# First chunk of direct attention units in full-height matmuls, 18 direct units for 20, and a new price for zeros in the planner

## Chip, cores and metric

The kernel runs on one core of a Trainium2 chip. The metric is the device time of one execution, in microseconds (us). The engines are PE (TensorE: matmuls; PEld is its weight loads), DVE (VectorE), ACT (ScalarE), POOL (GpSimd) and SP (SyncE, which issues the DMAs).

## The reference

Three layers follow one another: causal attention in blocks of 64, a mixing layer with squared ReLU, and a gated layer with a product over time. All data is float32. Cut to what matters:

```python
def _attn_ref(q, k, v):                       # q, k, v: (4, 8, 576, 64)
    scores = (1.0 / np.sqrt(D)) * np.matmul(q, k.transpose(0, 1, 3, 2))
    mask = (pos[:, None] // 64) >= (pos[None, :] // 64)
    scores = np.where(mask, scores, -1000000000.0)
    attn = softmax(scores)
    return np.matmul(attn, v)

def _moe_ref(x, mu_k, mu_r, w_k, w_v, w_r):   # x: (4, 576, 512), d_ff 1024
    xk = mu_k * x + (1.0 - mu_k) * x_prev
    xr = mu_r * x + (1.0 - mu_r) * x_prev
    k = np.maximum(xk @ w_k, 0.0)
    return sigmoid(xr @ w_r) * (k * k @ w_v)

def _moe2_ref(x, w_in, g_ln, w_sg, b_sg, w_out):
    u, v = split(gelu(x @ w_in))
    v_s = np.einsum('ts,bsd->btd', w_sg, layernorm(v) * g_ln) + b_sg[None, :, None]
    return x + (u * v_s) @ w_out
```

## The kernel before

**Units.** Attention is cut into 64 units: one batch and head, and either its first 320 queries (kind LO, chunks of 64, 128 and 128 queries) or its last 256 (kind HI, two chunks of 128). `CH0`, `CHN` and `CHE` give each chunk's first query, its number of queries, and the keys it can see. Units 0 to 15 are LO of batches 0 and 1, units 16 to 31 HI of the same; then the same for batches 2 and 3. A unit goes through three steps on PE: `emit_S` (scores, into the banks SA, SB or M), `emit_T` (128 by 128 transposes of the softmaxed scores P, into T) and `emit_PV` (product with V, into O). Between them DVE takes maxima (`stats`) and sums (`rr`), ACT scales (`nb`), takes exponentials (P) and copies T out (PH, PL).

**Direct and split units.** A unit n below `DIRECT` is direct: its scores and its value product are float32 matmuls, each of which the chip runs as two passes on PE, so that a float32 matmul stands twice in the trace. The mask is in two extra rows of q and k (66 rows; 128 in the first four units). Its output comes with queries as rows, is scaled by DVE into `otmp`, and for each pair of heads is transposed back by PE (`T<-ident,otmp`). All other units are split: q, k, v and P are cut into two float32r parts (ACT copies the high part, POOL or DVE subtracts), a score takes two one-pass matmuls, the value product ten for HI, and its output needs no transpose back. The first chunk of a LO unit has 64 queries. Rows 64 to 127 of its P are zeroed once at the start.

**The rest.** A moe1 matmul (`M<-xh,w`, `xl`, `kh`, `kl`, 288 columns, two passes of every three by the high part) needs weights that were loaded and converted on ACT, DVE and POOL (`w_split`; tiles u, th, w). In the opening moe1 can only take the channels of batch 0 whose heads are done.

**Order.** The program first lists all operations, then `Plan.schedule` plays them through a model with a duration per operation (`takes`, `preload`) and always takes for an engine the ready operation of lowest rank. Rank is the place in the list plus a bias: `MB` for mixing, `CB` for weight conversion, `SB` for softmax steps, `EV` for copies out of T, `XV` for attention outputs; lower goes earlier. A load of weights on SP waits while the model's DMA backlog is above `BACKLOG` ns. `LEFT` conversions are left for the moe1 loop. The order that comes out is fixed: on the chip each engine runs its list in that order and waits where it must. All engine instructions stand in the profile under line 596, so they are told apart by tiles.

**Fillers.** Where the model sees PE idle for over 300 ns in the first two layers, it puts matmuls of zeros into the list: a plain filler (`O<-calm 64x128`, one pass) when no group of matmuls is open in O, otherwise zeros that are added to the open group (`O<-calm 128x64`, float32, two passes). How many fit is gap over price; the price of one was

```python
f = (n / 2.4 + 6) * x          # n = 128 for a filler, 4 * 64 for zeros; x is 1 or 2
```

They do no work for the result, and once in the list PE runs all of them, needed or not.

Of the kernel before, what the change touches and what calls it, by code (L numbers as in the profile page):

```python
# [9 lines left out]
F32 = mybir.dt.float32  # L10
# [10 lines left out]
CH0 = [0, 64, 192, 320, 448]  # L21
CHN = [64, 128, 128, 128, 128]
# [54 lines left out]


FILL = 128
BACKLOG = 6000  # L80
MORE = 20.0
FILL_DUTY = 1.0
COLD_DUTY = 1.0
# [253 lines left out]
class Plan:  # L337
# [77 lines left out]
    def play(self, rings):  # L415
# [8 lines left out]
        order, opened, began = [], 0, 0.0  # L424
# [42 lines left out]
        while True:  # L467
            best = None
            for e in soon:
# [3 lines left out]
                if ripe[e]:  # L473
                    t = free[e]
# [8 lines left out]
            t, e = best  # L483
# [25 lines left out]
            if e == "NONE":  # L509
                op.run, op.end = (t, t), t  # L510
                if filler and filler.alts[0][2]["out"].tile.pool in op.alts[0][1]:
                    filler = None
            elif op.alts[i][1] == "dma_start":
                a = op.alts[i][2]
                v = next(x for x in a.values() if isinstance(x, View))
                rows = v.shape[0]
                size = v.cols * rows * 4 if not v.tile.dram else v.cols * 4
                t = max(t, lanes.pop(0) + 40)
                if e == "SP":
                    free[e] = t + 375  # L520
                dma = max(t + 1400, dma) + size / (250.0 if rows != 66 else 172.0)
                op.run, op.end = (t, t + 375), dma + 150
                lanes.append(op.end)
            else:
                busy, d, port = takes(e, *op.alts[i][1:])
                if e != "PE":
                    busy, d = busy + MORE, d + MORE
                s = t
                if e == "PE":
                    gap = t - free[e]  # L530
                    s = t = max(t, began + preload(op.alts[i][1], op.alts[i][2]) * (2.0 if gate.slow else 1.0))
                    a = op.alts[i][2]
                    if filler and self.filler_from <= t and gap > (100 if gate.slow else 300):
                        x = gate.step(free[e])
                        more, n = filler, FILL
                        if opened:
                            more, n = zeros(group) if group["out"].cols <= FILL else None, 4 * group["out"].cols
                        f = (n / 2.4 + 6) * x
                        room = gap - max(0, self.filler_from - free[e])
                        k = int(room * COLD_DUTY / f if x > 1 else (room - 100) * (FILL_DUTY if gate.share(t) > AMPLE else 1.0) / f) if more else 0  # L540
                        at = max(free[e], self.filler_from)
                        for _ in range(k):
                            order.insert(len(order) - 1, (more, 0))
                            gate.add(at, min(t, at + n / 2.4 * x))
                            at += f
                    if filler and "out" in a and a["out"].tile is filler.alts[0][2]["out"].tile:
                        opened += bool(a.get("start")) - bool(a.get("stop"))
                        group = a
                    x = gate.step(t)
                    fn, v, ins = op.alts[i][1], a.get("out", a.get("_0")), a.get("lhsT", a.get("_1"))  # L550
                    cols = (v.cols if fn == "matmul" else 60) * (4 if ins.tile.dt == F32 else 1) * ins.shape[0] / 128 / 2.4
                    gate.add(t, t + min(busy, cols) * x)
                    d += busy * (x - 1)
                    busy *= x
                if port:
                    o = "POOL" if e == "DVE" else "DVE"
                    s = max(t, lock[o])
                end = max(s + d, t + d)
                free[e] = max(s + busy, end - (d - busy))
                if port:  # L560
                    lock[e] = end - (150 if e == "DVE" else 0)
                op.run, op.end = (s, free[e]), end
                if e == "PE":
                    began = s
# [34 lines left out]
WHO = dict(oN="A", wl="P", wc="V", Q="A", K="A", Ql="P", Kl="P", V="A", Vl="P", PH="A", O="A", xh="A", xl="P", kh="A", kl="P",  # L599
           X="A", Xl="V", vh="V", vl="V", gU="P", gh="A", gl="V", sg="A", sl="V", R2="A", R="A", P="V", PL="V")  # L600
ALT = 200.0
MB = -300
CB = -200
SB = 0
EV = -200
XV = -200
LO, HI = 0, 1
CHUNKS = [[0, 1, 2], [3, 4]]
TOKENS = [(0, 320), (320, 576)]
# [19 lines left out]
]  # L629


DIRECT = 20
PADDED = 4
SEATS = [("SA", "SBa"), ("M", "M"), ("SBb", "SA"), ("M", "M"), ("SBa", "SBb"), ("SA", "SBa"), ("SBb", "SA"), ("SBa", "SBb"),
         ("SA", "SBa"), ("SBb", "SA"), ("SBa", "SBb"), ("SA", "SBa"), ("SBb", "SA"), ("SBa", "SBb"), ("SA", "SBa"), ("SBb", "SA")]
# [5 lines left out]
W1 = 21  # L641
UT = 2
CONV = 4
LEFT = 12
X0_AT = 0.55
CONV2 = 2

# [6 lines left out]
def fused_kernel(ctx: ExitStack, tc: tile.TileContext, first, later, qkv_lo, qkv_hi, mu,  # L654
# [48 lines left out]
    def mm(out, lhsT, rhs, start=False, stop=False):  # L703
        op = nc.tensor.matmul(out=out, lhsT=lhsT, rhs=rhs, start=start, stop=stop)
        t = out.tile
        if start and t in stopped:
            op.preds[stopped[t].n] = stopped[t]
        if stop:
            stopped[t] = op
# [170 lines left out]
    def emit_S(n):  # L880
        b, h, kind = units[n]
        order.need(("sp", n))
        Q, K, KL = splits.pop(n)
        chunks = CHUNKS[kind]
        if n < DIRECT and kind == LO:
            (sa, ka), (sb, kb) = [ptile(t, 512, PS_BUFS.get(t, 1)) for t in SEATS[n]]
            P = spots[n % 3]
        else:
            (sa, ka), (sb, kb) = ptile("SA", 512, 1), ptile("SB", 1024, 1)
            P = [(pbuf[1 - n % 2], o) for o in POFF]  # L890
        stc = {0: sa[:, 0:64], 1: sa[:, 64:256], 2: sb[:, 0:320], 3: sa[:, 0:448]}
        if kind == HI:
            stc[4] = sb[:, 224:800]
        skc = [ka, ka, kb, ka, kb]
        probs[n] = P
        pe(score_ns(n))
        mx, sm = smax[n % 4], ssum[n % 4]
        t0, t1 = TOKENS[kind]
        nb = atile([128, 5], F32, "nb", 4)
        rr = atile([128, 5], F32, "rr", 4)  # L900
        for c in chunks:
            q0, m, e, st = CH0[c] - TOKENS[kind][0], CHN[c], CHE[c], stc[c]
            for k0, k1 in PIECES[c]:
                o = st[0:m, k0:k1]
                if n < DIRECT:
                    mm(o, Q[:, q0:q0 + m], K[:, k0:k1], start=True, stop=True)
                    continue
                mm(o, Q[:, q0:q0 + m], K[:, k0:k1], start=True)
                mm(o, q2[n % 2][:, CH0[c]:CH0[c] + m], KL[:, k0:k1], stop=True)

        def red(cs):
            for c in cs:
                m, e, st = CHN[c], CHE[c], stc[c]
                nc.vector.tensor_reduce(out=mx[0:m, c:c + 1], in_=st[0:m, 0:e], axis=AX.X, op=ALU.max)
            s = slice(cs[0], cs[-1] + 1)
            nc.scalar.activation(out=nb[:, s], in_=mx[:, s], func=AF.Copy, scale=-0.125)

        def exp(cs):
            for c in cs:
                m, e, st, (p, po) = CHN[c], CHE[c], stc[c], P[c]  # L920
                nc.scalar.activation(out=p[0:m, po:po + e], in_=st[0:m, 0:e], func=AF.Exp,
                                     scale=0.125, bias=nb[0:m, c:c + 1], accum_out=sm[0:m, c, 0:1])

        def norm():
            cs = slice(chunks[0], chunks[-1] + 1)
            nc.vector.tensor_reduce(out=rr[:, cs], in_=sm[:, cs], axis=AX.X, op=ALU.add)
            nc.vector.reciprocal(out=rr[:, cs], in_=rr[:, cs])
            if n < DIRECT:
                scales[n] = rr
                return  # L930
            for c in chunks:
                m, e, (p, o) = CHN[c], CHE[c], P[c]

                p, r = p[0:m, o:o + e], rr[0:m, c:c + 1]
                plan.add(*[("scalar", "activation", dict(out=p, in_=p, func=AF.Copy, scale=r)) if w == "A" else
                           ("vector", "tensor_scalar", dict(out=p, in0=p, scalar1=r, scalar2=None, op0=ALU.mult,
                                                            op1=ALU.add, accum_out=junk[0:m, c:c + 1]))
                           for w in WHO["P"]])

        parts = [[0, 1, 2]] if kind == LO else [[3], [4]]  # L940
        t = 0
        for cs in parts:
            w = sum(CHE[c] for c in cs)
            sk = [skc[c] for c in cs]
            at(t, plan.rank(SB, lambda cs=cs: red(cs)), *sk)
            t += 1.1 * w
            at(t + 100, plan.rank(SB, lambda cs=cs: exp(cs)), *sk, ("P", n))
        at(t + 1.2 * w + 500, plan.rank(SB, norm), ("N" if n < DIRECT else "P", n))
# [39 lines left out]
    def direct_PV(n):  # L988
# [29 lines left out]
        t, tk = ptile("T", 512, 2)  # L1018
        t0, t1 = TOKENS[kind]
        for i, c in enumerate(chunks):  # L1020
            m = CHN[c]
            nc.tensor.transpose(t[:, CH0[c] - t0:CH0[c] - t0 + m], o[0:m, i, :], ident[0:m, 0:m])
        x = new_xt(b, h)
        at(0, plan.rank(XV, lambda: copy("O", x[:, 1 + t0:1 + t1], t[:, 0:t1 - t0])), tk, ("x", b, kind))

# [582 lines left out]
```

## Time and profile before

| | |
|---|---|
| median of 3 timed runs | 694.78 us (694.05 to 695.16) |
| the profiled execution | 693.84 us |
| its span, first to last instruction | 691.9 us |
| PE busy | 684.7 us, 99% of the span |
| PEld (weight loads) busy | 658.2 us, 95% |
| DVE, ACT, POOL busy | 450.8, 453.8, 308.6 us |
| matmul instructions on PE | 5074, with 136 fillers and 54 passes of zeros |

PE counts as busy from a matmul's start to its modelled end, so a busy PE can still be standing while its array empties; the starts of the weight loads show that better. The 1.9 us between span and time lie outside the program's instructions.

### The profile page before, as it was taken

How to read it: one execution, taken by the hardware profiler on the slowest of the kernel's cores; microseconds unless marked ns; L12 is line 12 of the kernel's file. 1: busy time of each engine (PE TensorE's matmuls, PEld its weight loads, DVE VectorE, ACT ScalarE, POOL GpSimd, SP SyncE). 2: the span in 40 equal slices, each digit the busy share in tenths (PEclk: the TensorE clock that was granted, in tenths of full speed). 3: DMA queues.
4: the chain of work that ended last, by engine and by line, in shares of the span. 5: the costliest groups of instructions: out<-in, count | busy, mean ns of one | idle time of the engine just before them, and what ended most of it. 6: DMA issues, size and time to landing. Idle time of an engine off the chain costs nothing.

```text
span 691.9 us, 14054 instructions
## 1 busy us (share of the span) xinstructions
PE 684.7 (99%) x5074; PEld 658.2 (95%) x5074; DVE 450.8 (65%) x1141; ACT 453.8 (66%) x1287; POOL 308.6 (45%) x374
## 2 busy tenths in 40 slices
PE   8999999999999999999999999999999999999998
PEld 6989989999999999999999999999999998998998
DVE  4767787257877766766776877686988257256233
ACT  5779877797998898998898898583452131132120
POOL 4345544665575566667677564240234032032031
PEclk9999999999999999999999999999999999999999
DMA  8564122234322323334332410633900300300102
GB/s 269 203 219 159 35 77 78 86 124 133 110 75 75 115 85 102 89 103 135 96 103 98 137 47 1 240 107 105 323 1 17 121 1 9 129 1 10 61 1 69
DMA packets 34821, 68.24 MB, mean 99 GB/s; under 512 B 6048, under 2 KB 20640, under 8 KB 34752
## 3 DMA queue, kind: packets, MB, share of 16 engines
q1 hardware_dynamic: 34608, 67.34, 30.1%
q8 instruction: 40, 0.66, 0.4%
q14 instruction: 29, 0.24, 0.1%
q10 hardware_dynamic: 144, 0.00, 0.0%
HBM read 54.75 MB, written 9.44 MB: 93 GB/s over the span
## 4 chain that ended last, share of the span: by engine, by line
PE 95%; DVE 2%; ACT 2%; DMA 0%; issue 0%; POOL 0%; POOLq 0%; ACTq 0%
PE M L596 49%; PE O L596 19%; PE T L596 10%; PE V L596 7%; PE SB L596 5%; PE SA L596 5%; ACT P L596 1%; DVE th L596 1%; DMA kh<-first_dram 0%; DVE stats L596 0%; DVE u L596 0%; ACT PH L596 0%; DVE otmp L596 0%; ACT otmp L596 0%; DVE o L596 0%
## 5 line engine op out<-in xcount | busy, mean ns | idle before, releaser
L596 PE MATMUL M<-xh,w 128*128 128x288 f32 x704 | 166.8, 305 | 0.1
L596 PEld LDWEIGHTS M<-xh,w 128*128 128x128 f32 x704 | 119.6, 188 | 1.0 <-ACT R L596 0.3
L596 PE MATMUL M<-xl,w 128*128 128x288 f32 x352 | 104.4, 297 | 0.0
L596 PE MATMUL M<-kh,w 128*128 128x288 f32 x432 | 104.0, 307 | 0.0
L596 POOL TENSOR_TENSOR xl<-t,xh 128x288 fp32r<-128x288 f32 x64 | 53.2, 832 | 58.9 <-ACT xh L596 55.7
L596 POOL TENSOR_TENSOR gt<-gt,U 128x288 f32<-128x288 f32 x32 | 29.5, 925 | 102.1 <-DVE gt L596 52.7
L596 PE MATMUL T<-ident,P 128*128 128x128 f32 x480 | 74.3, 274 | 0.3 <-ACT P L596 0.3
L596 PEld LDWEIGHTS M<-kh,w 128*128 128x128 f32 x432 | 73.6, 188 | 1.0 <-issue 0.6
L596 DVE TENSOR_TENSOR PL<-T,PH 128x320 fp32r<-128x320 f32 (+3 forms) x116 | 61.8, 543 | 17.4 <-ACT PH L596 16.5
L596 ACT ACTIVATE PH<-T 128x384 fp32r<-128x384 f32 (+4 forms) x138 | 63.7, 479 | 12.3 <-PE T L596 11.6
L596 POOL TENSOR_TENSOR kl<-R,kh 128x288 fp32r<-128x288 f32 x64 | 53.6, 840 | 32.4 <-ACT kh L596 31.3
L596 PEld LDWEIGHTS M<-xl,w 128*128 128x128 f32 x352 | 66.3, 188 | 0.3
L596 PE MATMUL M<-kl,w 128*128 128x288 f32 x216 | 63.8, 296 | 0.0
L596 PEld LDWEIGHTS T<-ident,P 128*128 128x128 f32 x480 | 58.0, 141 | 3.1 <-ACT P L596 0.8
L596 ACT ACTIVATE U<-M 128x288 f32<-128x288 f32 x32 | 13.2, 412 | 69.9 <-PE M L596 69.9
L596 DVE TENSOR_SCALAR_CACHE_REDUCE P<-P,rr 128x448 f32<-128x448 f32 (+3 forms) x104 | 58.2, 582 | 0.6
L596 POOL TENSOR_TENSOR k<-qkv,K 64x576 fp32r<-64x576 f32 (+1 forms) x44 | 53.7, 1221 | 4.4 <-ACT K L596 2.3
L596 PE MATMUL O<-gh,w 128*128 128x288 f32 x256 | 51.7, 294 | 0.2 <-DVE o L596 0.2
L596 PE MATMUL M<-XHL,w 128*128 128x288 f32 x384 | 51.7, 294 | 0.0
L596 PEld LDWEIGHTS M<-XHL,w 128*128 128x128 f32 x384 | 51.2, 188 | 0.1
L596 POOL TENSOR_TENSOR Q<-qkv,Q 64x256 fp32r<-64x256 f32 (+1 forms) x44 | 35.0, 794 | 33.2 <-ACT Q L596 20.0
L596 PE MATMUL O<-PH,V 128*128 128x256 f32 (+2 forms) x188 | 47.3, 279 | 0.0
(186 smaller groups left out, 1891.1 us busy)
## 6 DMA issues: line engine op xcount, KB each, us to landing
qkv<-qkv_hi_dram SPq DMA_DIRECT2D x28, 576.0 KB, 3.7
qkv<-qkv_lo_dram SPq DMA_DIRECT2D x16, 416.0 KB, 3.1
x2d<-th SPq DMA_DIRECT2D x32, 144.0 KB, 3.1
X<-x2d SPq DMA_DIRECT2D x4, 1152.0 KB, 5.6
outT_dram<-o SPq DMA_DIRECT2D x32, 144.0 KB, 1.8
w<-w_k_dram SPq DMA_DIRECT2D x8, 512.0 KB, 8.7
w<-w_v_dram SPq DMA_DIRECT2D x8, 512.0 KB, 4.3
w<-w_in_dram SPq DMA_DIRECT2D x8, 512.0 KB, 5.5
```

The costliest lines, as they stand in the source:

```text
L596: getattr(getattr(self.nc, e), fn)(*pos, **{k: real(x) for k, x in a.items() if k[0] != "_"})
```

## The change

The first chunk of a direct LO unit multiplies 128 queries instead of its own 64 (the 64 further rows of scores are not used), and its output is transposed back as 128 by 128 instead of 64 by 64; the extra columns are overwritten by the next chunk's. `DIRECT` falls from 20 to 18, so units 18 and 19 (HI, batch 0, heads 2 and 3) become split. In the planner zeros of this form cost at least 220 ns. Five biases, the DMA backlog and `LEFT` get other values, by which the whole order on all engines comes out anew.

```diff
-BACKLOG = 6000
+BACKLOG = 7500
...
-                        f = (n / 2.4 + 6) * x
+                        f = max(n / 2.4 + 6, 220.0 if opened and group["lhsT"].tile.dt == F32 and group["out"].shape[0] > 64 else 0) * x
...
-MB = -300
-CB = -200
-SB = 0
-EV = -200
-XV = -200
+MB = -200
+CB = -350
+SB = 200
+EV = -50
+XV = -100
...
-DIRECT = 20
+DIRECT = 18
...
-LEFT = 12
+LEFT = 14
...
                 if n < DIRECT:
-                    mm(o, Q[:, q0:q0 + m], K[:, k0:k1], start=True, stop=True)
+                    mm(st[:, k0:k1], Q[:, q0:q0 + 128], K[:, k0:k1], start=True, stop=True)
...
         for i, c in enumerate(chunks):
-            m = CHN[c]
-            nc.tensor.transpose(t[:, CH0[c] - t0:CH0[c] - t0 + m], o[0:m, i, :], ident[0:m, 0:m])
+            nc.tensor.transpose(t[:, CH0[c] - t0:CH0[c] - t0 + 128], o[:, i, :], ident)
```

Three places show how the order moves. The first is PE's list in the opening, around the scores of unit 5 (`SA<-qkv`) and the value product of unit 3 (`O<-kl,PL`); before:

```order
L596 MATMUL SA<-qkv 64x64
L596 MATMUL SA<-qkv 128x192
L596 MATMUL O<-calm 128x64 x8
L596 MATMUL M<-xh,w 128x288 x2
L596 MATMUL O<-kl,PL_315 128x64
L596 MATMUL O<-kl,PL_276 128x64
L596 MATMUL O<-kl,PL_315 128x64 x2
```

and now:

```order
L596 MATMUL SA<-qkv 128x64
L596 MATMUL SA<-qkv 128x192
L596 MATMUL O<-calm 128x64
L596 MATMUL O<-kl,PL_311 128x64
L596 MATMUL O<-kl,PL_278 128x64
L596 MATMUL O<-kl,PL_311 128x64 x2
L596 MATMUL T_167<-ident,P_88 128x128 x3
L596 MATMUL O<-calm 64x128 x18
```

The score has 128 rows, eight zeros have become one, two moe1 matmuls went later, and a run of 18 plain fillers stands after the next transposes. The second place is PE's list ahead of the scores of unit 7 (`SB<-qkv`), whose q, k and v are loaded into a buffer that unit 4's value product frees; before:

```order
L596 MATMUL O<-calm 64x128 x15
L596 MATMUL O<-qkv,PL_541 128x64 x2
L596 MATMUL O<-qkv,PL_543 128x64
L596 MATMUL O<-qkv,PL_541 128x64
L596 MATMUL O<-qkv,PL_543 128x64 x2
L596 MATMUL M<-xh,w 128x288
L596 MATMUL SB<-qkv 64x64
```

and now:

```order
L596 MATMUL O<-calm 64x128 x20
L596 MATMUL T_167<-ident,P_88 128x128 x3
L596 MATMUL O<-qkv,PL_507 128x64 x2
L596 MATMUL O<-calm 128x64
L596 MATMUL O<-qkv,PL_536 128x64
L596 MATMUL O<-qkv,PL_507 128x64
L596 MATMUL O<-qkv,PL_536 128x64 x2
L596 MATMUL O<-calm 64x128 x71
L596 MATMUL SB<-qkv 128x64
```

In place of one moe1 matmul a run of 71 fillers now stands right ahead of unit 7's scores. The third place is DVE's list just before it takes the maxima of the same unit 7 (`stats<-SB`), where `u` and `th` are steps of weight conversion; before:

```order
L596 TENSOR_REDUCE rr<-sums 128x3
L596 RECIPROCAL rr<-rr 128x3
L596 SCALAR_TENSOR_TENSOR u<-w,u 128x512
L596 TENSOR_SCALAR u<-u 128x512
L596 SCALAR_TENSOR_TENSOR u<-w,u 128x512
L596 SCALAR_TENSOR_TENSOR t_538<-xT,mu_t,t_538 128x288
L596 SCALAR_TENSOR_TENSOR u<-w,u 128x512
L596 TENSOR_TENSOR otmp<-O,rr 128x3x64
L596 TENSOR_REDUCE stats<-SB 64x1
```

and now:

```order
L596 TENSOR_TENSOR otmp<-O,rr 128x3x64
L596 TENSOR_SCALAR u<-u 128x512 x2
L596 SCALAR_TENSOR_TENSOR u<-w,u 128x512
L596 TENSOR_SCALAR u<-u 128x512
L596 SCALAR_TENSOR_TENSOR u<-w,u 128x512 x2
L596 TENSOR_SCALAR th<-th 128x512
L596 SCALAR_TENSOR_TENSOR u<-w,u 128x512
L596 TENSOR_REDUCE rr<-sums 128x3
L596 RECIPROCAL rr<-rr 128x3
L596 TENSOR_TENSOR otmp<-O,rr 128x3x64
```

The sums of a unit (`rr<-sums`), which free its output, now stand behind eight conversion steps in a row. Counted over the whole program, PE's list goes from 5074 passes to 5083: 69 more fillers (136 to 205), 42 fewer passes of zeros (54 to 12), 36 fewer passes of direct value products and 12 fewer of direct scores, 12 and 20 more of split scores and value products, and 2 fewer transposes back.

## Rows read from the trace of the kernel before

**Rows 1.** The profile's page: granted clock in 40 slices, 9 is 90% or more
```profile
PEclk9999999999999999999999999999999999999999
```

**Rows 2.** Two stretches: busy us (count) of PE, PEld, DVE, ACT, POOL; clock; DMA
```profile
0.00:62.00 62.00, 59.09 (x466) 51.39 (x466) 39.41 (x110) 44.98 (x141) 25.39 (x46) 1.00 0.70 233
62.00:120.00 58.00, 58.00 (x420) 52.49 (x420) 43.53 (x102) 47.51 (x142) 27.81 (x28) 1.00 0.19 55
```

**Rows 3.** Waits in the first 62 us: us in total, times, longest
```profile
DVE otmp L596 <- PE O L596: 6.1, 7, 2.2
...
DVE stats L596 <- PE SB L596: 4.5, 5, 1.9
...
ACT PH L596 <- PE T L596: 3.4, 4, 1.8
ACT xT L596 <- PE T L596: 3.4, 4, 1.1
```

**Rows 4.** Weight loads around a 64-query score: start us, us, what [idle before]
```profile
18.05 0.14 PEld L596 LDWEIGHTS T<-ident,P 128*128 128x128 f32 x1
...
18.36 0.19 PEld L596 LDWEIGHTS SA<-qkv 66*64 66x64 f32 x2 [0.17 <-issue]
...
18.61 0.19 PEld L596 LDWEIGHTS SA<-qkv 66*128 66x128 f32 x1
```

**Rows 5.** Weight loads: a transpose, then scores of 128 queries on 66 rows
```profile
15.54 0.14 PEld L596 LDWEIGHTS T<-ident,P 128*128 128x128 f32 x1
...
15.64 0.19 PEld L596 LDWEIGHTS SB<-qkv 66*128 66x128 f32 x1
...
15.64 0.30 PEld L596 LDWEIGHTS SB<-qkv 66*128 66x128 f32 x2
```

**Rows 6.** Weight loads around one first-chunk transpose back
```profile
36.09 0.14 PEld L596 LDWEIGHTS T<-ident,P 128*128 128x128 f32 x1
...
36.35 0.14 PEld L596 LDWEIGHTS T<-ident,otmp 64*128 64x128 f32 x1
...
36.72 0.14 PEld L596 LDWEIGHTS T<-ident,P 128*128 128x128 f32 x1
```

**Rows 7.** Timeline of PE: one direct score of 288 keys; direct value products
```profile
96.59 0.65 PE L596 MATMUL SB<-qkv 66*128 66x288 f32 x2
97.08 0.78 PE L596 MATMUL O<-qkv,PL 128*128 128x64 f32 x6
...
134.68 2.12 PE L596 MATMUL O<-qkv,PL 128*128 128x64 f32 x18
```

**Rows 8.** Timeline of PE: scores of a split unit; value product of one
```profile
132.85 0.45 PE L596 MATMUL SA<-K,Q 128*128 128x448 f32 x1
...
133.88 0.30 PE L596 MATMUL M<-xh,w 128*128 128x288 f32 x1
...
150.75 0.28 PE L596 MATMUL O<-PH,V 128*128 128x256 f32 x1
...
151.81 0.28 PE L596 MATMUL O<-PL,V 128*128 128x256 f32 x1
```

**Rows 9.** Zeros on PE: count | busy us, mean ns | idle before
```profile
L596 PE MATMUL O<-calm 128*128 128x64 f32 x54 | 6.8, 272 | 0.0
```

**Rows 10.** Timeline around a run of zeros
```profile
28.60 2.57 PE L596 MATMUL O<-calm 128*128 128x64 f32 x22
...
29.19 0.47 ACT L596 ACTIVATE PL<-T 128x384 f32<-128x384 f32 x1
...
31.00 1.06 PE L596 MATMUL O<-qkv,PL 128*128 128x64 f32 x8
...
32.09 0.36 DVE L596 TENSOR_TENSOR otmp<-O,rr 128x192 f32<-128x192 f32 x1 [2.17 <-PE O L596]
```

**Rows 11.** A run of plain fillers
```profile
25.96 1.05 PE L596 MATMUL O<-calm 128*64 128x128 f32 x14
```

**Rows 12.** VectorE's longest step on weights in the first 62 us
```profile
L596 DVE SCALAR_TENSOR_TENSOR u<-w,u 128x512 int32<-128x512 int32 x12 | 8.9, 748 | 0.0
```

## The prediction

> **What bounds the kernel now.** I read the granted clock first: it is full in all 40 slices [rows 1], so no time hides in a slow TensorE. Then the table by stretches. From 62 to 120 us PE is busy for all 58.00 us, and in the first 62 us for 59.09 [rows 2], while DVE and ACT have 39.41 and 44.98. PE's list is run in order, so the end of the program moves with two things only: how long PE needs for its list at its own pace, and how long it stands for others. In the opening both matter, because fillers make PE look busy where the planner expected it to stand. The waits there show which engine really leads: DVE and ACT stood 6.1, 4.5, 3.4 and 3.4 us for PE (17.4 in these four alone) [rows 3]. From about 62 us on, anything taken out of PE's list is gained at the end unless a new wait takes its place.
>
> A matmul's busy time is of no use for pricing PE, since successive ones overlap. I price by distances between starts.
>
> **The first chunk of scores.** Where a 64-query score follows a transpose, the transpose's weight load starts at 18.05, the score's first at 18.36 after 0.17 us of idle, and the first load of the 192-key score behind it at 18.61 [rows 4]: 0.56 us for three loads (the transpose and two passes). Without a change of shape loads follow each other at 0.10 to 0.11: 15.54, 15.64, and the second of the pair 0.11 later (0.30 less 0.19), and these last are scores of 128 queries on 66 rows straight behind a transpose [rows 5]. With 128 queries the three loads should take 0.33. That is 0.23 us less, 16 times (one per LO unit of batches 0 and 1): 3.7 us. A wider load costs something too: the two narrow ones start some 0.06 us apart (0.19 for both, each 0.13 to 0.14 long), against 0.11; that is already inside the 0.33. Ends of the range: 3.7, and a loss of 1.7 if the idle time stays (32 loads, 0.055 each).
>
> **The transposes back.** From the load of the transpose before (36.09) over the 64-row one (36.35) to the load after the 128-row ones (36.72) is 0.63 us for three loads [rows 6], against 0.33. Here the first load began early, behind a filler, so I take 0.25 and not 0.30. Eight pairs of heads: 2.0 us.
>
> **Two units fewer are direct.** A direct HI unit has a score of 288 keys twice, at 0.49 each (96.59 to 97.08), and one of 448, by columns 0.76; its 18 value passes go at 0.112 each ((2.12 - 0.78)/12) [rows 7], 2.01; and half of a pair's two transposes back, 0.11. Sum 3.86 us. A split unit needs 1.03 for its scores (132.85 to 133.88) and 1.18 for ten value passes (150.75 to 151.81 for nine, and 0.12) [rows 8], 2.21. The difference, 1.65, counts twice: 3.3 us. What the two units add on ACT, DVE, POOL and SP (copies and subtractions of q, k, v, P, and two small DMAs) is what 28 later HI units do already. It lies beside moe1 matmuls that PE can do meanwhile, while DVE is free for 14.5 of 58 us [rows 2]; I cost it at nothing. Without that cover it would be one more step ahead of each unit's scores, some 0.75 us each if it is as long as the step in [rows 12].
>
> **Fillers and zeros.** The trace has 54 passes of zeros [rows 9]; 42 go. In a run of 22 they start 0.11 apart (28.60 to 31.00), and that run shows what they cost when too many: the copy PL that the next product needs was done at 29.66 (29.19 and 0.47), but the product started at 31.00, and DVE stood 2.17 us for it [rows 10]. Plain fillers go at 0.062 ((1.05 - 0.24)/13) [rows 11]; 69 come. So 4.6 us less and 4.3 more: 0.3 us less. The fillers now stand where the planner sees the waits, the largest run, 71 or 4.4 us, ahead of unit 7's scores.
>
> **The sum.** 3.7 + 2.0 + 3.3 + 0.3 = 9.3 us by which PE's list is shorter at its own pace. From the profiled execution, 693.84, that leaves 684.5; its time is 0.94 below the median of 694.78, so 685.5 against the median.
>
> **What is given back.** About 5.5 of these 9.3 us (scores and most transposes back) lie in the opening, where PE then reaches its meeting points earlier than DVE and ACT may be ready. How much comes back as waits no row shows; the bounds are none and all 5.5. I set it by who waited for whom there: PE's share is the time that its list holds for waiting, 136 fillers at 0.062 and 54 zeros at 0.11, 14.3 us, against the 17.4 us that others waited for PE, so 45%, or 2.5 us. This is an estimate. Net gain 6.8 us: 688.0.
>
> **The biases and the backlog** move work between neighbours on every engine but neither add nor remove any. By the order, one more weight load (11 for 10) stands ahead of unit 7's on SP. I cost them at nothing, with the rivals below as their price.
>
> **Rivals.**
> *All of it is gained, and the overrun with it.* For: DVE and ACT were waiting for PE more than the reverse [rows 3], and the run of zeros above wasted 1.3 us on the chain to unit 7's load. Against: the 71 fillers say that the planner expects a wait at the same place. 9.3 to 11 us less: 684 to 685.5, with one more such overrun 683. Chance 0.25.
>
> *The opening is held by others.* If the first units go at the pace of DVE and ACT with their weight conversions, all 5.5 us come back and only 3.8 stay: 691. For: DVE's 39.4 and ACT's 45.0 of 62 us are not far from a dependent chain's limit. Against: the same waits. Chance 0.18.
>
> *The full-height score gains nothing.* If what PE waited for came from the 66 rows and not the 64 columns, the 3.7 go, the wider loads cost 1.7, and 3.9 less about 1 of waits stays: 691.9. Against it stand the 66-row loads without any gap [rows 5]. Chance 0.04. The Trainium skill, "TensorE: Matmul & The Clock Gate", section "LDWEIGHTS (loading the stationary operand)", has a load cost its columns over 1.2 GHz, so 53 ns for 64 and 107 for 128; by that rule alone the change lengthens 32 loads by 1.7 us. The same skill's "TensorEngine Tiling (Array Packing)", section "Key Properties", says that changing the tiling mode drains the array, which speaks for the other reading. The trace agrees with both at once, 0.06 against 0.11 between loads and 0.17 of idle at the change [rows 4, 5]; only for the plain fillers, also 64 columns wide, is no such gap seen: the first load in [rows 6] stands behind one and has no idle time.
>
> *Slower: conversions ahead of the softmax.* DVE now has eight conversion steps in a row ahead of a unit's sums, ACT likewise. One of the long ones takes 0.75 us [rows 12]. PE is in order, so what it stands for at one unit delays everything behind. The gain of 9.3 is used up by 12 such steps that nothing covers, less than one for each of the 16 LO units. One for each is 12 us: 697.5. Against: conversions must be done before moe1 can use PE, so early ones also remove waits; and PE's list holds fillers at these places. Chance 0.08.
>
> *Nothing to be seen,* gains and waits cancelling: 693.4 to 696.2. Chance 0.05.
>
> **How the numbers follow.** The forecast, 685.5 to 690, has 0.40 and is the likeliest; its time is 688.0. A measurement of this kernel tells about 0.2%, 1.4 us, from no change. Faster by more are the forecast and the first three rivals, 0.87, less 0.01 for their upper tails: 0.86; within 0.2% 0.06; slower 0.08. The range reaches down to the full gain with one overrun and up through the opening held by others and the idle score: 682.5 to 692.
>
> **What would show it.** The 66-row scores have one shape, with loads 0.11 apart and no idle time ahead of the first chunk. The transposes back start 0.11 apart. The first split HI scores come two units earlier. By the scores of unit 15, the last LO unit of batch 1, PE is about 3 us ahead; by the end of attention about 3 more. If the waits for PE grow in the first 62 us, the estimate of 2.5 was too large; if PE's own waits for ACT P, DVE otmp or the load of qkv pass 4 us, the opening is held by others. Any slice with a granted clock below 1.00 would make it all wrong.

## The result, and the profile after

The changed kernel takes 687.58 us (median of 4 runs, 686.53 to 687.72) against 694.97 for the kernel before: a ratio of 0.9892, 95% interval 0.9877 to 0.9907, or 7.4 us less. Forecast were 688.0 and 682.5 to 692. The profiled execution took 687.72, its span is 686.0.

The page after, busy shares and granted clock:

```profile
PE 678.2 (99%) x5083; PEld 657.9 (96%) x5083; DVE 459.7 (67%) x1155; ACT 458.5 (67%) x1294; POOL 316.4 (46%) x380
...
PEclk9999999999999999999999999999999999999999
```

Two stretches of it (busy us of PE, PEld, DVE, ACT, POOL; clock; DMA):

```profile
0.00:62.00 62.00, 58.05 (x494) 52.61 (x495) 43.09 (x115) 45.78 (x140) 26.09 (x47) 1.00 0.68 233
62.00:120.00 58.00, 57.47 (x435) 54.65 (x435) 39.15 (x98) 47.27 (x140) 30.91 (x32) 1.00 0.24 72
```

The clock is full throughout, as before [rows 1]. PE is still the bound: 678.2 of 686.0 us. In the first 62 us it is busy less (58.05 for 59.09) and DVE more (43.09 for 39.41) [rows 2].

Weight loads after, around the first chunk of unit 5's scores (start us, us, what):

```profile
18.46 0.14 PEld L596 LDWEIGHTS T<-ident,P 128*128 128x128 f32 x1
...
18.57 0.19 PEld L596 LDWEIGHTS SA<-qkv 66*128 66x128 f32 x1
...
18.68 0.19 PEld L596 LDWEIGHTS SA<-qkv 66*128 66x128 f32 x1
...
18.79 0.19 PEld L596 LDWEIGHTS SA<-qkv 66*128 66x128 f32 x1
```

The transpose's load starts at 18.46, the two of the score at 18.57 and 18.68, the first of the 192-key score at 18.79: 0.33 us for three and no idle time, for 0.56 with 0.17 of idle [rows 4]. A transpose back with what follows it, on PE's timeline after:

```profile
33.29 0.49 PE L596 MATMUL T<-ident,otmp 128*128 128x128 f32 x3
33.62 0.27 PE L596 MATMUL T<-ident,P 128*128 128x128 f32 x1
```

and the same place before:

```profile
36.13 0.29 PE L596 MATMUL T<-ident,P 128*128 128x128 f32 x1
36.35 0.64 PE L596 MATMUL T<-ident,otmp 64*128 64x64 f32 x3
36.83 0.38 PE L596 MATMUL T<-ident,P 128*128 128x128 f32 x2
```

Three matmuls follow each other at 0.11 now (33.29 to 33.62). Before, the four from 36.13 to 36.83 took 0.70, where 0.44 would be the pace: 0.26 less, as priced (0.25), though [rows 6] hold four loads and not three as the prediction counted.

The waits of the opening after:

```profile
ACT nb L596 <- DVE stats L596: 7.4, 4, 4.5
...
DVE otmp L596 <- PE O L596: 3.9, 6, 1.5
DVE stats L596 <- PE SB L596: 3.4, 4, 1.6
...
ACT xT L596 <- PE T L596: 1.1, 2, 0.8
```

DVE and ACT wait less for PE now (3.9, 3.4, 1.1 for 6.1, 4.5, 3.4) [rows 3]; the first line, ACT's wait for DVE's maxima, comes back below. PE's timeline ahead of unit 7's scores:

```profile
37.57 4.48 PE L596 MATMUL O<-calm 128*64 128x128 f32 x71 [0.45 <-DVE otmp L596]
41.89 0.38 PE L596 MATMUL SB<-qkv 66*128 66x64 f32 x2
```

The 71 fillers run from 37.57 for 4.48 us, and the scores start at 41.89. Then comes what the total hides. Where does unit 15, the last LO unit of batch 1, start its scores, when in both orders 138 moe1 matmuls are done? On PE's timeline before:

```profile
88.05 0.27 PE L596 MATMUL SB<-qkv 66*64 66x64 f32 x1
```

and after:

```profile
88.59 0.22 PE L596 MATMUL SB<-qkv 66*128 66x64 f32 x1
```

At 88.05 and at 88.59. These are single executions, and in the first 14 us they differ even where PE's list is the same. Unit 4's first scores, the first to be made of `qkv`, stand here in the changed kernel:

```profile
14.56 0.33 PE L596 MATMUL SB<-qkv 66*128 66x64 f32 x2
```

and here in a kernel of the experiments with the same list up to that place:

```profile
13.23 0.33 PE L604 MATMUL SB<-qkv 66*128 66x64 f32 x2
```

The two are 1.33 us apart, so a difference of that size between two starts of unit 15 says nothing; its distance from unit 4's scores (13.77 before) says more. That is 74.28 before and 74.03 after. The opening has become shorter by 0.25 us, although it holds nearly all of the faster scores and transposes. Nearly the whole gain came behind it. The experiments ask why.

### The profile page after: what moved, and what is told of

Its sections match the earlier page's. It is cut to its first block, busy times and chain, and to the rows that moved or that the text cites. A ratio compares the mean times of both kernels' runs of the same rounds, so it can differ in the third digit from the quotient of the medians.

```text
span 686.0 us, 14157 instructions
## 1 busy us (share of the span) xinstructions
PE 678.2 (99%) x5083; PEld 657.9 (96%) x5083; DVE 459.7 (67%) x1155; ACT 458.5 (67%) x1294; POOL 316.4 (46%) x380
## 4 chain that ended last, share of the span: by engine, by line
PE 94%; DVE 3%; ACT 1%; issue 0%; DMA 0%; POOL 0%; DVEq 0%; POOLq 0%
PE M L596 48%; PE O L596 19%; PE T L596 10%; PE V L596 7%; PE SB L596 5%; PE SA L596 5%; DVE u L596 1%; DMA kh<-first_dram 0%; ACT P L596 0%; POOL gt L596 0%; DVE otmp L596 0%; DVE va L596 0%; DVE stats L596 0%; DVE sgl L596 0%; DVE vb L596 0%
## 5 line engine op out<-in xcount | busy, mean ns | idle before, releaser
L596 PE MATMUL M<-xh,w 128*128 128x288 f32 x704 | 164.7, 304 | 0.0
L596 PE MATMUL M<-kh,w 128*128 128x288 f32 x432 | 101.8, 304 | 0.0
L596 DVE TENSOR_TENSOR PL<-T,PH 128x320 fp32r<-128x320 f32 (+3 forms) x122 | 64.7, 544 | 27.8 <-ACT PH L596 26.6
L596 PE MATMUL T<-ident,P 128*128 128x128 f32 x480 | 76.9, 274 | 0.1
L596 DVE TENSOR_SCALAR_CACHE_REDUCE P<-P,rr 128x448 f32<-128x448 f32 (+3 forms) x108 | 60.2, 589 | 0.8
L596 POOL TENSOR_TENSOR k<-qkv,K 64x576 fp32r<-64x576 f32 (+1 forms) x46 | 56.8, 1234 | 3.8 <-ACT K L596 1.0
L596 PE MATMUL O<-PH,V 128*128 128x256 f32 (+2 forms) x198 | 50.7, 278 | 0.0
```

What stands on the lines that cost most here:

```text
L596: getattr(getattr(self.nc, e), fn)(*pos, **{k: real(x) for k, x in a.items() if k[0] != "_"})
```

## The experiments

The theory under test is that of the prediction: PE's list at its own pace, less what the opening gives back in waits. Its rivals: the opening is held by the other engines, so nothing of the full-height chunk is gained; and the new biases, which the prediction had cost at nothing, move time themselves. Times are medians; the kernel before ran beside each group (694.8 to 695.4). The 95% intervals of the ratios are 0.6 to 1.7 us to either side. "List price" is what the prediction's distances between starts give. "Unit 15" is the start of its scores in the trace; "from unit 4" counts from the start of unit 4's.

**The shape alone, the order held.** The planner works as in the one kernel, and only when the instructions are issued is the shape of the other used. In the changed kernel, with 64 queries again:

```diff
-    mm(st[:, k0:k1], Q[:, q0:q0 + 128], K[:, k0:k1], start=True, stop=True)
+    mm(st[:, k0:k1], Q[:, q0:q0 + 128], K[:, k0:k1], start=True, stop=True).shape_as = (
+        dict(out=o, lhsT=Q[:, q0:q0 + m]) if m < 128 else {})
...
+            a = {**a, **op.shape_as} if op.shape_as else a
             if e == "gate":
```

and the same for the transposes back; in the kernel before the other way round.

> The order of the changed kernel is kept on every engine; only the first chunk's scores and transposes back are issued with 64 queries again. List theory (PE's list, fillers and all, sets the pace of the opening too): the 16 scores and 8 transposes cost 5.7 us more at list pace, so about 693.3. Prediction's estimate (some of it comes back as waits): about 3.2 us more, 690.8. Others theory (DVE, ACT and loads hold the opening, since unit 15's scores started no earlier after the change): 0 to 1 us more, 687.6 to 688.6.

> The order of the kernel before is kept on every engine; only the first chunk's scores and transposes back are issued with 128 queries. List theory: 5.7 us less than before, 689.3. Prediction's estimate: 3.2 us less, 691.8. Others theory: 0 to 1 us less, 694 to 695.

Measured: 690.76 with 64 queries in the new order (0.9935 of before, 0.9922 to 0.9949), 3.2 us more than the changed kernel. In the old order 128 queries give 690.85 (0.9932, 0.9919 to 0.9945), 4.1 us less than before. So the shape is worth 3.2 or 4.1 of its 5.7 us, two values that the noise does not tell apart: from unit 4 to the last matmul the two pairs of traces differ by 3.01 and 2.74. The rest, 2.5 or 1.6 by the medians, would be what comes back as waits (the estimate was 2.5); no row measures it directly. The shape does shorten the opening. Unit 15 in the old order with 128 queries:

```profile
85.16 0.26 PE L597 MATMUL SB<-qkv 66*128 66x64 f32 x1
```

and in the new order with 64:

```profile
90.74 0.27 PE L597 MATMUL SB<-qkv 66*64 66x64 f32 x1
```

85.16 for 88.05 in the old order, 88.59 for 90.74 in the new one. With equal shapes, then, the new order is 2.7 us (64 queries) or 3.4 us (128) later at unit 15, from unit 4 (14.05 in the new order with 64, 14.15 in the old with 128) 2.4 or 3.0. "Held by others", as the whole account, falls; something in the order takes the time.

**Fillers left out, the order held.**

```diff
+            if op.n < 0 and length > 60:
+                continue
             if e == "gate":
```

`op.n` is below 0 for fillers and zeros, `length` that of their run; the second kernel has the condition without the length.

> The order of the changed kernel is kept, but the run of 71 fillers ahead of unit 7's scores is left out (it adds nothing to the result). List theory: these fillers are an overrun (unit 7's load was issued at 29.6 us, the fillers ran from 37.6 to 41.9), so 4.3 us less, 683.3. Others theory: PE stands there instead, no change, 687 to 688.

> The order of the changed kernel is kept, but all 205 fillers and 12 passes of zeros are left out (they add nothing to the result). List theory: 8 us or more less, 680. Others theory: PE idles where the fillers stood, 686 to 688. Third possibility: with PE idle the granted clock falls below 1.00 in the opening and it is slower, 690 or more.

Measured: 687.83 without the 71 (0.9891, 0.9876 to 0.9905), no change. Unit 7's scores now start at once, and the saved time is lost a moment later:

```profile
35.65 1.31 PE L604 MATMUL SB<-qkv 66*128 66x64 f32 x6
...
41.32 0.83 PE L604 MATMUL M<-xh,w 128*128 128x288 f32 x2 [3.34 <-ACT xh L604]
41.95 2.12 PE L604 MATMUL O<-calm 128*64 128x128 f32 x18
```

35.65 instead of 41.89, but at 41.32 PE stands 3.34 us for ACT's copy `xh`, and behind that the clock is at its lower level:

```profile
42.00:44.00 2.00, 2.00 (x20) 2.00 (x19) 1.66 (x5) 1.16 (x6) 2.00 (x1) 0.50 1.01 399
```

so that the next 18 fillers take 2.12 us, for 1.24 in the changed kernel. These 71 fillers were not an overrun; they lay where ACT was late. Without any filler it is slower than the changed kernel, 690.98 (0.9932, 0.9908 to 0.9956), and the clock says why:

```profile
20.00:22.00 2.00, 1.02 (x6) 0.62 (x6) 1.67 (x5) 1.90 (x6) 0.24 (x1) 0.99 1.02 401
22.00:24.00 2.00, 2.00 (x11) 1.88 (x9) 0.73 (x3) 1.25 (x6) 1.78 (x2) 0.50 1.03 401
...
20.00:40.00 20.00, 17.28 (x93) 15.56 (x93) 12.52 (x36) 14.56 (x40) 5.75 (x5) 0.72 0.48 174
40.00:62.00 22.00, 18.92 (x78) 16.03 (x79) 15.68 (x39) 14.85 (x43) 10.86 (x9) 0.56 0.63 221
```

From 20 to 22 us PE is busy for only 1.02 of 2 us, and then the granted clock falls from 2.4 to 1.2 GHz; its means are 0.72 and 0.56 from 20 to 40 and from 40 to 62 us. PE's busy 17.28 of 20 and 18.92 of 22 us there do not contradict this: at the lower clock each matmul lasts longer, so PE looks full (2.00 of 2 from 22 to 24 us). The eight executions of this kernel show it again: they took 687.57 to 695.23 us, the shortest two with a mean clock of 0.987 and 0.988, the longest with 0.975. Against that, the 16 us that fillers and zeros take in the opening of the changed kernel are cheap.

**Two units fewer direct.** `DIRECT` alone, in the kernel before and back in the changed one, planned anew:

```diff
-DIRECT = 20
+DIRECT = 18
```

> The kernel before with 18 direct units alone, planned anew. Prediction: 3.3 us less, 691.6. Rival: the two further split units wait for their copies and subtractions and bring 1 us or less, 694 to 695.

> The changed kernel with 20 direct units, planned anew. Prediction: 3.3 us more than the changed kernel, 690.9. Rival: 1 us more or less, 688.5.

Measured: 695.99 for the kernel before with 18, no gain (1.0011, 1.0002 to 1.002). The changed kernel with 20 takes 691.55 (0.9946, 0.9933 to 0.9958), 4.0 us more than with 18. The same edit is worth 4.0 in one order and nothing in the other. In the latter the cover was gone. One stretch in the old planner's order with 18:

```profile
88.00:130.00 42.00, 40.30 (x318) 36.60 (x317) 32.53 (x76) 34.06 (x93) 26.34 (x24) 1.00 0.40 116
```

and with 20, the kernel before:

```profile
88.00:130.00 42.00, 42.00 (x306) 38.64 (x306) 26.98 (x60) 30.26 (x82) 19.46 (x19) 1.00 0.27 82
```

With 18 units DVE, ACT and POOL are busy 32.53, 34.06 and 26.34 of the 42 us, for 26.98, 30.26 and 19.46, and PE is no longer full (40.30). In PE's list there are 60 fillers and 16 zero passes behind unit 15 for 18 and 4, 5.1 us more by the trace. So the planner saw PE standing for the split units' preparation, and what it put there is more than the 3.3 that the units save. That is a reading of the list; no run takes the preparation away. Nor do the fillers alone tell which plan gains: in the last experiment 36 fillers and 8 zero passes stand behind unit 15 with 18 units and 22 and 2 with 20, and the two units still bring 3.1.

**The biases.**

```diff
-BACKLOG = 6000
+BACKLOG = 7500
...
-MB = -300
-CB = -200
-SB = 0
-EV = -200
-XV = -200
+MB = -200
+CB = -350
+SB = 200
+EV = -50
+XV = -100
...
-LEFT = 12
+LEFT = 14
```

> The kernel before with the new biases, backlog and LEFT alone. Prediction costs them at nothing: 694 to 696. Rival: with conversions first the opening is later by 2.7 us (unit 15's scores in the run with 64 queries in the new order stood 2.7 us later than before) and this stays: 697.6. Second rival: the same 2.7 us come back after unit 15, since less is left to do and to wait for: 694 to 695, with unit 15 later by 2 us or more in the trace.

> The changed kernel with the old biases, backlog and LEFT, planned anew. Prediction: no change, 687 to 688.5. Rival (conversions first cost the opening 2.7 us for good): 685. Second rival (they pay later): 688 to 690, with unit 15's scores earlier by 2 us or more than in the changed kernel.

Measured: the kernel before with the new ones 696.33 (1.0014, 1.0005 to 1.0023), 1.0 us more; the changed kernel with the old ones 684.38 (0.9845, 0.9832 to 0.9859), 3.2 us less than the changed kernel and the best of all. Unit 15 in the first:

```profile
93.63 0.27 PE L596 MATMUL SB<-qkv 66*64 66x64 f32 x1
```

and in the second:

```profile
82.77 0.23 PE L596 MATMUL SB<-qkv 66*128 66x64 f32 x1
```

93.63 for 88.05, and 82.77 for 88.59: the new values put unit 15 off by 5.6 and 5.8 us; from unit 4 (15.39 in the first, 13.86 in the second) it is 4.0 and 5.1. ACT's wait for DVE's maxima goes with them. In the first 62 us it is 7.4 in the changed kernel (above) and this with the new values in the kernel before:

```profile
ACT nb L596 <- DVE stats L596: 7.5, 4, 4.2
```

and this with the old ones, in the kernel before and in the changed one:

```profile
ACT nb L596 <- DVE stats L596: 5.3, 2, 4.2
...
ACT nb L596 <- DVE stats L596: 5.2, 2, 4.4
```

Part of the delay comes back: from unit 15 to the last matmul the changed kernel needs 593.9 us, with the old values 596.3. The fillers and zeros behind unit 15 make up all of this 2.3 us and more: by the trace they take 0.98 us in the changed kernel and 3.82 with the old values.

Which values do it? The old backlog and LEFT alone:

```diff
-BACKLOG = 7500
+BACKLOG = 6000
...
-LEFT = 14
+LEFT = 12
```

> The changed kernel with the old backlog and LEFT (6000, 12), but the new five biases, planned anew. If the later opening came from loads (one more weight load ahead of unit 7's): unit 15's scores at 83 to 85 us and 684.5 to 685.5. If it came from the order of conversions before softmax steps: no earlier than 87 us, and 686.5 to 688.5.

Unit 15 stood at 87.52, with 120 moe1 matmuls done instead of 138. So what puts unit 15 off is the ranks, not the backlog or `LEFT`. At the end it takes 694.27 (0.9991, 0.9982 to 0.9999), 6.7 us more than the changed kernel, where the expectation was 686.5 to 688.5. This does not weigh the ranks, for at the seam to the third layer this order has a stall of its own, as does the next kernel. PE's waits there:

```profile
PE M L596 <- POOL xl L596: 3.5, 1, 3.5
```

and the stretch:

```profile
460.00:480.00 20.00, 16.54 (x106) 15.82 (x105) 13.65 (x24) 7.82 (x15) 5.25 (x3) 0.91 0.09 29
```

PE stands 3.5 us, and the mean clock from 460 to 480 us is 0.91. POOL's subtraction `xl`, for which PE waits, takes 4.17 us there (4.18 in the next kernel); in the changed kernel and the one before the longest such step takes 1.35. Why it does is open. The two kernels with the stall are those that join the new ranks, late in the program, with the old backlog and `LEFT`. The ranks changed by place, old ones until the first eight units are done and new ones after:

```diff
     take(conv, len(conv) - LEFT)
+    globals().update(MB=-200, CB=-350, SB=200, EV=-50, XV=-100)
```

> The changed kernel with the old five biases, backlog and LEFT until the first eight units are done, and the new five biases from there on, planned anew. If the new biases cost the opening and help later: unit 15's scores at 83 to 85 us as with the old ones, and 1 to 2 us less than 684.4 at the end, 682.5 to 683.5. Rival: what they help later was only what they had put off, 684 to 685.

690.3 (0.9929, 0.9912 to 0.9945). Unit 15 came at 83.53, as with the old values, but the same stall at the seam (3.5 us, clock 0.83 from 460 to 480 us) hides what the rest is worth. One of its six executions kept the full clock and took 687.60, still more than 684.38. The forecast of 682.5 to 683.5 failed, and whether the new ranks help later stays open.

**The price of zeros, and the units once more,** both on the best kernel. First the old price:

```diff
-f = max(n / 2.4 + 6, 220.0 if opened and group["lhsT"].tile.dt == F32 and group["out"].shape[0] > 64 else 0) * x
+f = (n / 2.4 + 6) * x
```

> The changed kernel with the old biases, backlog and LEFT and also the old price of zeros, planned anew; it has 32 more passes of zeros than the same kernel with the new price (62 for 30) and as many fillers. If PE's list sets the pace of the opening with the old biases: 3.5 us more than that kernel's 684.4, 687.9. Rival: the zeros stand where PE would wait anyway, 684.5 to 685.5.

686.39 (0.9877, 0.9864 to 0.9889), 2.0 us more for 32 passes; of the 3.5 that they take at list pace some 60% shows at the end.

> The changed kernel with the old biases, backlog and LEFT, and 20 direct units, planned anew. If two split units are worth their 3.3 us once the first chunk has 128 queries and zeros have their price: 3 to 4 us more than 684.4, 687.5 to 688.5. If their copies and subtractions cost as much as they save under the old biases too, as in the kernel before with 18 alone: 684 to 685.

687.48 (0.9888, 0.9871 to 0.9904), 3.1 us more than with 18.

## Why the prediction came out right

One chain of kernels leads from the one to the other, so its steps must add up to the result; what it tells is their sizes, each to about 1 us: before 694.97; 128 queries in its order 690.85 (-4.1); 18 direct units and a plan that knows the shape 686.39 (-4.5); the price of zeros 684.38 (-2.0); the new biases 687.58 (+3.2). In sum -7.4.

- **What bounds.** Right in the main: PE's list does. The shape taken alone moves the end by most of its list price. But 71 fillers, 4.4 us of the list, could go and nothing was gained, so in the opening the list alone does not set the pace.
- **The first chunk, 3.7 + 2.0.** Shown by the starts (0.33 us for three, at the score and at the transposes back) and by the two kernels with the order held: 3.2 and 4.1 net. "Given back, 2.5" fits both within the noise (2.5 and 1.6), but it came from a share (fillers of the whole program against waits of the first 62 us) and not from a mechanism, so its fit does not confirm the share.
- **Two units, 3.3.** 3.1 and 4.0 in the two new orders. The step "I cost it at nothing", with DVE's free time as cover, holds only there: in the old plan the edit alone brought nothing. The chain's -4.5 holds some 1.4 more than these 3.1, from planning anew with the known shape; no run takes that apart.
- **Fillers and zeros, 0.3.** The counts were right. The price alone, though, is worth 2.0 on the best kernel; the 69 fillers that hid this in the count come largely with the biases (76 more fillers up to unit 15 than with the old values).
- **The biases and the backlog, "I cost them at nothing",** is the step that failed. In the changed kernel they cost 3.2 us at the end and 5.1 by unit 15 from unit 4; in the kernel before 1.0 and 4.0. The rival "conversions ahead of the softmax" had named the place and the sign; it was too dear, since part comes back later. That conversions ahead of softmax steps are the mechanism is argued from DVE's order and fits ACT's longer waits for the maxima (7.4 and 7.5 for 5.2 and 5.3); the runs show only that the ranks, and not the backlog or `LEFT`, put unit 15 off.
- **"By the scores of unit 15, the last LO unit of batch 1, PE is about 3 us ahead"** was wrong: from unit 4 it is 0.25 ahead, for the same reason. That the end came out at 687.58 for a forecast of 688.0 is luck, for two misses nearly cancelled: without the biases the edits gain 10.6 us and not 6.8, and the biases take 3.2 of it.

Open: what each of the five ranks does, whether the conversions are their mechanism, and what makes POOL's step long at the seam.

## What to carry to other kernels

Price a shape change by the distance between weight loads, not by busy times: an idle 0.17 us ahead of a narrow matmul pointed to the edit, and the trace gave it before the run. A list of constants in a planner is an edit like any other: ask what each moves ahead of what, and test it alone, for a gain elsewhere can hide its loss. Compare places where equal work is done, not only the end, and count from a place behind the start, which differs between executions of one list.

## What was not expected of the hardware

Leaving out 17 us of fillers and zeros made the kernel slower, by the clock: it fell to 1.2 GHz behind 2 us in which PE was busy for 1.02, and was 0.56 on average from 40 to 62 us. PE's busy share there, 18.92 of 22, gives no hint of it, since a slow PE looks busy.

And narrow matmuls are not all alike. The float32 ones cost time at the change of shape: the scores of 64 columns, two passes each, stood idle for 0.17 us [rows 4], and a transpose back of 64 rows, one pass, took 0.26 us more. Those that the program makes of float32r, the fillers and the scores of the split units, change to 128 columns and back without idle time [rows 6]; the split units' narrow weight loads before, with the idle time in the last column:

```profile
L596 PEld LDWEIGHTS SA<-K,Q 128*64 128x64 f32 x16 | 2.2, 135 | 0.0
L596 PEld LDWEIGHTS SA<-k,q 128*64 128x64 f32 x16 | 2.1, 134 | 0.0
```

That the type decides it fits these rows; no run changes the type alone. The Trainium skill, "TensorEngine Tiling (Array Packing)", section "Key Properties", has every change of tiling mode drain the array; if 64 columns beside 128 are such a change, the trace agrees for the float32 scores, 0.17 us, and not for the fillers and split scores, 0.0.
